# Gated linear attention and a mixture of experts: group 0 instead of group 1 takes K and Q through DRAM, and two groups sum |W|² by accumulating transfers

## The chip, the cores and the metric

The kernel runs on one core of one Trainium2 chip. Its engines are TensorE (PE, matrix products), VectorE (DVE, elementwise), ScalarE (ACT, functions and copies), GpSimd (POOL) and SyncE (SP); POOL and SP issue DMA transfers here. The metric is the device time of one execution in microseconds (us), lower is better. Everything is float32 in SBUF; the two matrix products of the experts use split float32r operands.

## The reference

Part one is a recurrence with a complex decay, over B=4 sequences, H=8 heads, S=768 steps and D=48 channels. Part two is a skip gate and a mixture of eight experts over the 3072 tokens that result.

```python
mag = np.sqrt(a_re * a_re + a_im * a_im)
scale = np.minimum(mag, 0.999) / (mag + 1e-06)
a_re_n, a_im_n = (a_re * scale, a_im * scale)
for t in range(S):
    ar, ai = (a_re_n[:, :, t, :, None], a_im_n[:, :, t, :, None])
    new_re = ar * S_re - ai * S_im
    new_im = ar * S_im + ai * S_re
    kv = np.einsum('bhd,bhe->bhde', k[:, :, t], v[:, :, t])
    S_re, S_im = (new_re + kv, new_im)
    y[:, :, t] = np.einsum('bhd,bhde->bhe', q[:, :, t], S_re)
...
do_compute = x @ w_skip > 0
e_idx = np.argmax(xc @ w_gate, axis=1)
h = np.maximum(xc[mask] @ w1[e], 0.0)
y[mask] = gate_w[mask, None] * (h @ w2[e])
out[do_compute] = xc + y
```

Here x is y with heads side by side (3072 x 384), xc its rows with a positive skip score, gate_w the largest softmax probability, and w1, w2 have an inner width of 1024.

## The kernel before, in words

The 768 steps are cut into 6 chunks of 128 steps, and two chunks make a group (NG = 3). Within a chunk the state is not carried: W is the running product of the decays from the middle of the chunk outwards, both halves (64 steps each) and both chunks of a group at once in the 128 partitions (2 halves x 2 chunks x 32 pairs of sequence and head). So a group is 64 steps of a serial string of small DVE instructions, the chain: multiply by the decay (L371), add the two products (L380). L365 copies the first decay of a group. A group has 8 pieces of 8 steps each, 24 pieces in all.

Ahead of the chain, gates normalise the decays (ACT L258 to L267, DVE L262, L266, L316, L324). Behind it, a consumer turns each piece of W into the two operands of the chunk's products: K times W (nw, L443) on one side of the middle and K over W on the other, and the same of Q. The inverse is the conjugate over |W|², so ACT squares W into ws (L438); the sum of the two squares is formed; ACT takes the power of the sum (L459, L460), and DVE refines it and forms iw (L462, L464, L467, L470). The sum is formed on PE, by two products with the identity into PSUM (sw, L452), except for a group's last piece, where DVE adds (L457).

The products contract over the channels, so K and Q have to lie with channels in partitions. For groups 0 and 2 each piece's nw and iw are transposed on PE (tp, L533) and copied by ACT (L540) into the two qk tiles of the group. Group 1 is the spilled group: its nw and iw, both K and Q, are written by POOL to a scratch in DRAM (keep, L492), read back by SP in natural order (nat, L503), and transposed by whole heads on PE (turn, tu L518) with ACT copies of 512 elements (L520). For group 0 only K goes to DRAM, since the state update contracts over time and needs it in natural layout (nat, L506).

A unit is one sequence's 8 heads of one chunk (c, b); 24 in all. It has scores (pa, PE L590, 16 products), mask (at, DVE L612, 2), the outputs (py, PE L667 and L670), the state update from natural K and V (ps, PE L656; RX on DVE; st by ACT L639), the copy and the gate's projection (px L675), and now and then a routing pass (small DVE instructions, then indirect scatters by POOL, xs). The spilled group's units read q and k after turn, and their K from the same natural tile.

The order of the instructions is written by generators under a class Order that keeps virtual times for the engines: chain, gates, consumers, units and weights each yield and are taken by priority and by lateness. The tile framework adds the waits and can hold an instruction on a buffer that is still read. The pools' buffer counts matter: qk has 2 buffers (a group's two tiles), nat and qkT 2 each. The consumers of group 1 go on at once; those of group 2, past the first piece, wait until 8 units are done, because their qk tiles reuse the buffers of group 0. After the attention come the routing's last pass and the experts.

The prediction counts work by stage and in the DVE order; "chain step" is the number of L380 instructions counted from the start (64 or 65 to a group, the last closing the group; 195 in all).

Of the kernel before, what the change touches and what calls it, by code (L numbers as in the profile page):

```python
# [9 lines left out]
F32 = mybir.dt.float32  # L10
# [4 lines left out]
ALU = mybir.AluOpType  # L15
# [4 lines left out]
B, H, S, D = 4, 8, 768, 48  # L20
DM = H * D
BH = B * H
C = 128
HC = 64
NCH = S // C
NG = NCH // 2
# [73 lines left out]
def vt(n, f=1.0):  # L100
    return (n / f + 65) / 0.96
# [8 lines left out]
class Kern:  # L110
# [229 lines left out]

    def chain(self, g):
        V = self.nc.vector
        qk = None
        if not self.spilled(g):
            qk = [self.qkp.tile([96, BH, 4, HC], F32, name=f"qk_{g}_{cc}", tag="qk") for cc in range(2)]
        self.QK[g] = qk
        prev = None
        for p in range(NP):
            i = g * NP + p
# [5 lines left out]
            n = LP + (1 if p == NP - 1 else 0)  # L355
# [33 lines left out]
    def consumers(self):  # L389
        while self.cons_done < NPC:  # L390
            g, u = divmod(self.cons_done, NP)
            if self.cq and (self.spilled(g) or u < 1 or self.units_done >= (g - 1) * 2 * B):
                yield from self.consume(*self.cq.pop(0))
            else:
                yield 0, 100

        self.rctx.close()
        self.m0 = self.pool(self.mctx, "m0", side="right")
        self.mr = self.pool(self.mctx, "mr", 2, side="right")
        self.t2 = self.pool(self.mctx, "t2", side="right")  # L400
        self.order.add(P_WEIGHTS, self.weights(0, self.m0), 3000)
# [30 lines left out]
    def consume(self, g, i, W, num, inv, jb, qk, wl):  # L432
# [13 lines left out]
        self.keep(g, nw, 1, 1, jb)  # L446
        yield o.wait(vt(2 * N), ts)
        w2, r0 = ws[:, :, 0], ws[:, :, 1]
        if wl is None:
            sw = self.ps_w.tile([128, LP, D], F32, name=f"sw_{i}", tag="sw")  # L450
            for c in range(2):
                nc.tensor.matmul(sw, self.ident, ws[:, :, c], start=(c == 0), stop=(c == 1))  # L452
            o.pe(1300, ts)
            cost = 0.0
        else:
            sw = w2
            V.tensor_tensor(w2, w2, r0, ALU.add)  # L457
            cost = vt(N)
# [9 lines left out]
        yield vt(N), 130  # L468
        iw = self.wk.tile([128, LP, 2, D], F32, name=f"iw_{i}", tag="nw")
        V.tensor_tensor(iw, bc(inv), Wm, ALU.mult)  # L470
        tq = self.trans(i, iw, 2, 1, jb, qk, vt(2 * N)) + 5000
        self.keep(g, iw, 1, 0, jb)
        self.keep(g, iw, 0, 1, jb)
        if wl is not None:
# [8 lines left out]

    def spilled(self, g):

        return g == 1

    def keep(self, g, src, side, q, jb):

# [5 lines left out]
    def nat(self, c, b):  # L495

        if c >= 2 * (NG - 1):
            return
        g, cc = divmod(c, 2)
        t = self.nats[c, b] = self.un.tile([C, H, 2, 2 * D], F32, name=f"nat_{c}_{b}", tag="nat")  # L500
        r = cc * BH + b * H
        if self.spilled(g):
            self.nc.sync.dma_start(t.rearrange("p h q d -> p (h q) d"),  # L503
                                   self.kq[g][r:r + H].rearrange("h q s d -> s (h q) d"))
        else:
            self.nc.sync.dma_start(t[:, :, 0], self.kq[g][r:r + H, 0].rearrange("h s d -> s h d"))  # L506

    def turn(self, c, b):

        nc = self.nc  # L510
        t = self.nats[c, b]
        qk = self.un.tile([96, H, 4, HC], F32, name=f"qkT_{c}_{b}", tag="qkT")
        for hh in range(2):
            hs = slice(hh * 4, hh * 4 + 4)
            for q in range(2):
# [83 lines left out]
    def unit(self, c, b):  # L599
# [88 lines left out]
            self.routes.append((self.lg_t, self.route1(c, b, lg, self.xa)))  # L688
        if c > 0:
            yield vt(768), 0  # L690
        nx = c * B + b + 2
        if nx < (c // 2 + 1) * 2 * B:
            self.nat(*divmod(nx, B))

# [8 lines left out]

    def units(self, g):
        self.nat(2 * g, 0)
        self.nat(2 * g, 1)
        self.unit_at(2 * g, 0)
        for cc in range(2):
            c = 2 * g + cc
# [169 lines left out]
    def attention(self):  # L879
        with ExitStack() as ctx:  # L880
# [1 line left out]
            P = lambda *a, **kw: self.pool(ctx, *a, **kw)  # L882
            self.rctx = ExitStack()
            self.ld, self.gt, self.wk = [self.pool(self.rctx, n, 2, side="right") for n in ("ld", "gt", "wk")]
            self.qkp, self.un, self.st = P("qk", 2), P("un", 2), P("st")
            self.ps_tp, self.ps_at = P("ps_tp", 2, space=PSUM), P("ps_at", 2, space=PSUM)
            self.ps_y, self.ps_s, self.ps_m = P("ps_y", 1, space=PSUM), P("ps_s", 1, space=PSUM), P("ps_m", 1, space=PSUM)
            self.ps_w = P("ps_w", 1, space=PSUM)
# [357 lines left out]
```

## Time and profile before

| | us |
|---|---|
| median of 3 runs | 538.61 |
| lowest, highest | 535.48, 540.12 |
| profiled execution, its own time | 543.87 |
| span of the profiled execution | 542.2 |

PE is busy 430.7 us of the span, DVE 412.1, ACT 291.8, POOL 88.3; the mean granted TensorE clock is 0.887. In a group row of the profile, "busy" is the union of a group's executions and the mean in ns that of one; PE's products overlap, so their pitch is shorter than their mean. A window row gives its bounds, its length, then for PE, PE's weight loads, DVE, ACT and POOL the busy us (and the instructions started), and last the granted TensorE clock, the share of the DMA engines and GB/s. In a waits row stand the total us, how many times, and the longest wait.

### The profile page before, as it was taken

Reading aid. Unit: us, or ns where it says so; the run is one execution under the profiler, and the core shown is the slowest. Engines: PE = TensorE matmul, PEld = TensorE weight load, DVE = VectorE, ACT = ScalarE, POOL = GpSimd, SP = SyncE. Lnnn points to the kernel's source line nnn. Section 1 sums busy time; section 2 is a strip of 40 time slices with the busy share of each in tenths; the row PEclk is TensorE's granted clock in tenths of the full one; section 3 lists DMA queues with packets and bytes.
Section 4 is the critical chain, followed back from the end, with each engine's and each line's share of the span. In section 5 each row is a group of like instructions: output and inputs, shape, how many; then the busy total and the mean of one; then the engine's idle time right before and its main releaser. Section 6 shows DMA issues by size and latency. Waiting matters only on the chain. (4 is left out here: it accounts for less than half of the span.)

```text
span 542.2 us, 10042 instructions
## 1 busy us (share of the span) xinstructions
PE 430.7 (79%) x3253; PEld 376.9 (70%) x3253; DVE 412.1 (76%) x1139; ACT 291.8 (54%) x658; POOL 88.3 (16%) x158
## 2 busy tenths in 40 slices
PE   0256446579989322899999998999998999999994
PEld 0134324479866201788778888998988999999994
DVE  2988999965999989789889847689469566866621
ACT  3657657714655554587778673332266454654410
POOL 4011011101132444000000300202112001120111
PEclk9966876667999765799999996799999999999998
DMA  4558777787988867858644325534659568666300
GB/s 85 113 113 179 176 151 169 159 163 178 230 196 195 197 152 168 186 113 194 135 112 110 96 67 179 145 113 119 219 175 312 189 209 273 182 196 226 105 20 28
DMA packets 160523, 85.72 MB, mean 158 GB/s; under 512 B 134491, under 2 KB 154463, under 8 KB 160464
## 3 DMA queue, kind: packets, MB, share of 16 engines
q1 hardware_dynamic: 155216, 70.93, 51.7%
q0 software_dynamic: 5248, 14.07, 9.6%
q8 instruction: 28, 0.46, 0.3%
q14 instruction: 31, 0.25, 0.1%
HBM read 61.84 MB, written 25.21 MB: 161 GB/s over the span
## 5 line engine op out<-in xcount | busy, mean ns | idle before, releaser
L452 PE MATMUL sw<-ws,ident 128*128 128x384 f32 x84 | 44.3, 664 | 37.9 <-ACT ws L438 37.9
L371 DVE TENSOR_TENSOR X<-W,ain 128x192 f32<-128x192 f32 x192 | 67.7, 352 | 2.9
L936 DVE TENSOR_TENSOR l<-r,h 128x768 fp32r<-128x768 f32 (+1 forms) x56 | 58.0, 1069 | 13.3 <-ACT h L935 13.2
L935 ACT CAST h<-r 128x768 fp32r<-128x768 f32 (+1 forms) x56 | 49.7, 925 | 17.6 <-DMA r<-in_moe_w_dram 12.7
L452 PEld LDWEIGHTS sw<-ws,ident 128*128 128x128 f32 x84 | 19.5, 257 | 50.6 <-issue 27.1
L1000 PE MATMUL ph<-xh,h 128*128 128x256 f32 x192 | 53.0, 282 | 0.6 <-issue 0.6
L1000 PE MATMUL ph<-xh,l 128*128 128x256 f32 x192 | 53.2, 282 | 0.0
L1002 ACT ACTIVATE hh<-ph 128x256 fp32r<-128x256 f32 x64 | 23.7, 382 | 53.8 <-PE ph L1000 53.8
L612 DVE TENSOR_TENSOR at<-pa,mask 128x512 f32<-128x512 f32 x48 | 32.7, 685 | 25.1 <-PE pa L590 21.4
L380 DVE TENSOR_TENSOR W<-X 128x96 f32<-128x96 f32 x192 | 48.7, 254 | 3.4
L1000 PE MATMUL ph<-xl,h 128*128 128x256 f32 x192 | 51.0, 281 | 0.0
L533 PE MATMUL tp<-ident,iw 128*96 128x128 f32 x128 | 23.6, 331 | 33.6 <-DVE iw L470 33.3
L1003 DVE SCALAR_TENSOR_TENSOR hl<-ph,hh 128x256 fp32r<-128x256 f32 x64 | 25.6, 418 | 29.2 <-ACT hh L1002 29.2
L540 ACT COPY qk<-tp 96x256 f32<-96x256 f32 x128 | 39.8, 369 | 11.4 <-PE tp L533 10.9
L1023 PE MATMUL po<-h,hh 128*128 128x384 f32 x128 | 43.8, 342 | 0.0
L739 POOL DMA_INDIRECT xs<-xa,sl x24 | 29.1, 1212 | 88.8 <-DVE l L936 20.5
L533 PEld LDWEIGHTS tp<-ident,iw 128*96 128x96 f32 x128 | 17.1, 151 | 37.9 <-issue 30.6
L1024 PE MATMUL po<-l,hh 128*128 128x384 f32 x128 | 43.3, 338 | 0.0
L667 PE MATMUL py<-at,vt 128*64 128x128 f32 x384 | 42.5, 298 | 0.0
L590 PE MATMUL pa<-qk 96*128 96x128 f32 x256 | 41.3, 316 | 1.0 <-DVE at L612 0.9
L1025 PE MATMUL po<-h,hl 128*128 128x384 f32 x128 | 39.5, 337 | 0.0
L590 PEld LDWEIGHTS pa<-qk 96*128 96x128 f32 x256 | 36.9, 222 | 3.2 <-PE py L670 1.1
(225 smaller groups left out, 1077.2 us busy)
## 6 DMA issues: line engine op xcount, KB each, us to landing
r<-in_moe_w_dram SPq DMA_DIRECT2D x24, 512.0 KB, 5.4
r<-in_moe_w_dram SPq DMA_DIRECT2D x32, 384.0 KB, 4.2
nat<-kq SPq DMA_DIRECT2D x8, 768.0 KB, 5.5
kq<-nw POOLq DMA_DIRECT2D x24, 192.0 KB, 3.4
kq<-iw POOLq DMA_DIRECT2D x24, 192.0 KB, 2.9
vt<-in_v_dram SPq DMA_DIRECT2D x24, 192.0 KB, 2.8
out_dram<-xa SPq DMA_DIRECT2D x24, 192.0 KB, 2.1
ain<-in_a_re_dram SPq DMA_DIRECT2D x90, 48.0 KB, 2.9
```

The lines of the kernel that those rows point to most:

```text
L371: V.tensor_tensor(X, prev.unsqueeze(1).to_broadcast([128, 2, 2, D]), windows(ain[:, j]), ALU.mult)
L380: self.cins = V.tensor_tensor(W[:, j, ::-1], X[:, :, 0], X[:, :, 1], ALU.add).ins
L452: nc.tensor.matmul(sw, self.ident, ws[:, :, c], start=(c == 0), stop=(c == 1))
L533: nc.tensor.transpose(tp[:, jj], src[:, s * 4 + jj], self.ident)
L540: nc.scalar.copy(o, tp[:, :, :, cc].rearrange("p j s b -> p b s j"))
L590: nc.tensor.matmul(pa[h // 4][:, h % 4], KT(h), QT(h), start=True, stop=True)
L667: PE.matmul(py[j * 64:j * 64 + 64, hp], vt_[:, 2 * hp + j], at[:, 2 * hp + j], start=True, stop=(c == 0))
L935: nc.scalar.copy(hi[:, ks], raw)
L936: nc.vector.tensor_tensor(lo[:, ks], raw, hi[:, ks], ALU.subtract)
L1000: pe = PE.matmul(ph, w[:, k, js], x[:, k], start=(n == 0), stop=(n == len(terms) - 1))
L1023: PE.matmul(po, hh[:, j, sl], w2h[:, j], start=(j == 0), stop=False)
L1024: PE.matmul(po, hh[:, j, sl], w2l[:, j], start=False, stop=False)
```

## The change

Group 0 becomes the spilled group, so its K and Q go through DRAM and are turned by whole heads, and group 1's pieces are transposed one by one. The pool of qk tiles has three buffers. Group 0 uses one of them (area): natural tiles lie in its first part, turned ones behind them, two of each. Groups 1 and 2 have the other two and then, for the second tile of group 2, the buffer that group 0's units have left or that chunk 2's units leave. The natural K of later units has a tile with a single buffer of its own, and is loaded one unit ahead instead of two. For the pieces of groups 1 and 2 the sum of the two squares is made by a transfer that POOL issues with addition at its target, ws onto ws; group 0 keeps PE's way. The delay of 5000 before the first units of a group is for the spilled group only, and the consumers of the last group go on after 12 units instead of 8.

```diff
--- before.py
+++ after.py
@@ -340,9 +340,12 @@
 
     def chain(self, g):
         V = self.nc.vector
-        qk = None
-        if not self.spilled(g):
-            qk = [self.qkp.tile([96, BH, 4, HC], F32, name=f"qk_{g}_{cc}", tag="qk") for cc in range(2)]
+        qk = [self.qkp.tile([128, BH * 4 * HC], F32, name=f"qk_{g}_{cc}", tag="qk")
+              for cc in range(1 if self.spilled(g) else 2)]
+        if self.spilled(g):
+            self.area, qk = qk[0], None
+        else:
+            qk = [t[0:96].rearrange("p (h k t) -> p h k t", h=BH, k=4) for t in qk]
         self.QK[g] = qk
         prev = None
         for p in range(NP):
@@ -389,7 +392,7 @@
     def consumers(self):
         while self.cons_done < NPC:
             g, u = divmod(self.cons_done, NP)
-            if self.cq and (self.spilled(g) or u < 1 or self.units_done >= (g - 1) * 2 * B):
+            if self.cq and (g < NG - 1 or u < 1 or self.units_done >= 3 * B):
                 yield from self.consume(*self.cq.pop(0))
             else:
                 yield 0, 100
@@ -446,7 +449,13 @@
         self.keep(g, nw, 1, 1, jb)
         yield o.wait(vt(2 * N), ts)
         w2, r0 = ws[:, :, 0], ws[:, :, 1]
-        if wl is None:
+        if g:
+
+            sw = w2
+            nc.gpsimd.dma_start(w2, r0, accum_op=ALU.add)
+            ts += 4000
+            cost = 0.0
+        elif wl is None:
             sw = self.ps_w.tile([128, LP, D], F32, name=f"sw_{i}", tag="sw")
             for c in range(2):
                 nc.tensor.matmul(sw, self.ident, ws[:, :, c], start=(c == 0), stop=(c == 1))
@@ -468,7 +477,7 @@
         yield vt(N), 130
         iw = self.wk.tile([128, LP, 2, D], F32, name=f"iw_{i}", tag="nw")
         V.tensor_tensor(iw, bc(inv), Wm, ALU.mult)
-        tq = self.trans(i, iw, 2, 1, jb, qk, vt(2 * N)) + 5000
+        tq = self.trans(i, iw, 2, 1, jb, qk, vt(2 * N)) + 5000 * self.spilled(g)
         self.keep(g, iw, 1, 0, jb)
         self.keep(g, iw, 0, 1, jb)
         if wl is not None:
@@ -483,7 +492,7 @@
 
     def spilled(self, g):
 
-        return g == 1
+        return g == 0
 
     def keep(self, g, src, side, q, jb):
 
@@ -497,19 +506,26 @@
         if c >= 2 * (NG - 1):
             return
         g, cc = divmod(c, 2)
-        t = self.nats[c, b] = self.un.tile([C, H, 2, 2 * D], F32, name=f"nat_{c}_{b}", tag="nat")
         r = cc * BH + b * H
         if self.spilled(g):
+            t = self.part(c, b, 0, H * 4 * D).rearrange("p (h q d) -> p h q d", h=H, q=2)
             self.nc.sync.dma_start(t.rearrange("p h q d -> p (h q) d"),
                                    self.kq[g][r:r + H].rearrange("h q s d -> s (h q) d"))
         else:
+            t = self.un.tile([C, H, 1, 2 * D], F32, name=f"kt_{c}_{b}", tag="kt", bufs=1)
             self.nc.sync.dma_start(t[:, :, 0], self.kq[g][r:r + H, 0].rearrange("h s d -> s h d"))
+        self.nats[c, b] = t
+
+    def part(self, c, b, o, n):
+
+        o += (c * B + b) % 2 * n
+        return self.area[:, o:o + n]
 
     def turn(self, c, b):
 
         nc = self.nc
         t = self.nats[c, b]
-        qk = self.un.tile([96, H, 4, HC], F32, name=f"qkT_{c}_{b}", tag="qkT")
+        qk = self.part(c, b, 2 * H * 4 * D, H * 4 * HC)[0:96].rearrange("p (h k t) -> p h k t", h=H, k=4)
         for hh in range(2):
             hs = slice(hh * 4, hh * 4 + 4)
             for q in range(2):
@@ -688,7 +704,7 @@
             self.routes.append((self.lg_t, self.route1(c, b, lg, self.xa)))
         if c > 0:
             yield vt(768), 0
-        nx = c * B + b + 2
+        nx = c * B + b + (2 if self.spilled(c // 2) else 1)
         if nx < (c // 2 + 1) * 2 * B:
             self.nat(*divmod(nx, B))
 
@@ -703,7 +719,8 @@
 
     def units(self, g):
         self.nat(2 * g, 0)
-        self.nat(2 * g, 1)
+        if self.spilled(g):
+            self.nat(2 * g, 1)
         self.unit_at(2 * g, 0)
         for cc in range(2):
             c = 2 * g + cc
@@ -882,7 +899,7 @@
             P = lambda *a, **kw: self.pool(ctx, *a, **kw)
             self.rctx = ExitStack()
             self.ld, self.gt, self.wk = [self.pool(self.rctx, n, 2, side="right") for n in ("ld", "gt", "wk")]
-            self.qkp, self.un, self.st = P("qk", 2), P("un", 2), P("st")
+            self.qkp, self.un, self.st = P("qk", 3), P("un", 2), P("st")
             self.ps_tp, self.ps_at = P("ps_tp", 2, space=PSUM), P("ps_at", 2, space=PSUM)
             self.ps_y, self.ps_s, self.ps_m = P("ps_y", 1, space=PSUM), P("ps_s", 1, space=PSUM), P("ps_m", 1, space=PSUM)
             self.ps_w = P("ps_w", 1, space=PSUM)
```

Three places show what stands where in the order. Names: tp a piece's transposes (the first number is the piece), tpe the transposed decays at a group's end, sw the sum on PE, tu turned natural K or Q (chunk, sequence, half of the heads, K or Q), pa scores, ps state product, py outputs, at masked scores; the last number is only a running one.

PE, before, from the end of group 0's transposes to the first units of chunk 0:

```order
L533 MATMUL tp_7_1_2_1045<-ident_59,iw_7_1036 96x128 x4
L452 MATMUL sw_8_1115<-ws_8_1108,ident_59 128x384 x2
L551 MATMUL tpe_0_1057<-ident_59,e_0_1055 96x128 x2
L590 MATMUL pa_0_0_0_1134<-qk_0_0_193 128x128 x4
L590 MATMUL pa_0_0_1_1135<-qk_0_0_193 128x128 x4
L656 MATMUL ps_0_0_1172<-vt0_164,nat_0_0_1129 96x48 x8
L590 MATMUL pa_0_1_0_1162<-qk_0_0_193 128x128 x4
L667 MATMUL py_0_0_1183<-at_0_0_1147,vt0_164 64x128 x4
```

PE, after, at the same place:

```order
L461 MATMUL sw_6_748<-ws_6_729,ident_59 128x384 x2
L567 MATMUL tpe_0_870<-ident_59,e_0_868 96x128 x2
L549 MATMUL tp_8_0_0_910<-ident_59,nw_8_908 96x128 x4
L549 MATMUL tp_8_1_0_917<-ident_59,nw_8_908 96x128 x4
L534 MATMUL tu_0_0_0_0_940<-ident_59,qk_0_0_193 96x128 x4
L534 MATMUL tu_0_0_0_1_946<-ident_59,qk_0_0_193 96x128 x4
L672 MATMUL ps_0_0_1035<-vt0_164,qk_0_0_193 96x48 x8
L534 MATMUL tu_0_0_1_0_952<-ident_59,qk_0_0_193 96x128 x4
L534 MATMUL tu_0_0_1_1_958<-ident_59,qk_0_0_193 96x128 x4
L606 MATMUL pa_0_0_0_965<-qk_0_0_193 128x128 x4
```

The transposes of group 0's pieces are gone; piece 8 of group 1 and the turning of unit 0_0 stand ahead of the first scores, and the turning of each next unit between the units' products.

DVE, before, the end of the chain:

```order
L371 TENSOR_TENSOR X_23_8_3658<-W_23_3542,ain_23_3151 128x192
L443 TENSOR_TENSOR nw_22_3498<-num_22_3331,W_22_3341 128x768
L380 TENSOR_TENSOR W_23_3542<-X_23_8_3658 128x2x48
L428 TENSOR_TENSOR wend_112<-es_2_3679 128x48
L470 TENSOR_TENSOR iw_22_3553<-inv_22_3332,W_22_3341 128x768
L612 TENSOR_TENSOR at_3_3_3486<-pa_3_3_0_3433,mask_72 128x512
L612 TENSOR_TENSOR at_3_3_3486<-pa_3_3_1_3434,mask_72 128x512
```

DVE, after, where the last unit of chunk 3 stands now (piece 21 of 0 to 23):

```order
L374 TENSOR_TENSOR X_21_1_3322<-W_21_3297,ain_21_2835 128x192
L479 TENSOR_TENSOR iw_19_3176<-inv_19_2850,W_19_2859 128x768
L383 TENSOR_TENSOR W_21_3297<-X_21_1_3322 128x2x48
L628 TENSOR_TENSOR at_3_3_3328<-pa_3_3_0_3207,mask_72 128x512
L628 TENSOR_TENSOR at_3_3_3328<-pa_3_3_1_3208,mask_72 128x512
L374 TENSOR_TENSOR X_21_2_3330<-W_21_3297,ain_21_2835 128x192
```

The masked products of unit 3_3 stood behind the last step of the chain; now two and a half pieces of the chain come after them.

POOL, after, in group 1 (before, the rows of L455 are not there):

```order
L501 DMA kq1_121<-iw_8_1072 64x768
L455 DMA ws_9_1170<-ws_9_1170 128x8x48
L501 DMA kq1_121<-nw_9_1172 64x8x96
L734 COPY xa_1_1449<-tok_101 128x4
L455 DMA ws_10_1334<-ws_10_1334 128x8x48
L237 MEMSET ain_15_1805 64x144
L501 DMA kq1_121<-iw_9_1312 64x768
L501 DMA kq1_121<-nw_10_1336 64x8x96
L455 DMA ws_11_1627<-ws_11_1627 128x8x48
```

The accumulating transfer of each piece stands in POOL's order between the writes of K to DRAM, and ACT's logarithm (L468) waits for it.

## The prediction

> **What bounds the kernel now.** I read the page's table of engines first, then the busy time by stage, then DVE's waits, and last the rows at the places that the change touches. The page's chain of waits is no help: it holds only the last output transfer. Over the whole run PE and DVE are nearly level:
>
> ```profile
> PE 430.7 (79%) x3253; PEld 376.9 (70%) x3253; DVE 412.1 (76%) x1139; ACT 291.8 (54%) x658; POOL 88.3 (16%) x158
> ```
>
> That average hides the stages. These windows are cut at the end of group 0's recurrence (93.9), where the first units begin (104.8), where the K and Q of group 1 are about to come back from DRAM (214.7), at the end of group 2's recurrence (311.3), at chunk 4's first masked product (326.7) and at the end of the attention (376); per engine they give busy microseconds:
>
> ```profile
> 12.60:104.80 92.20, 44.73 (x158) 29.89 (x159) 84.36 (x225) 61.02 (x156) 11.22 (x22) 0.73 0.69 148
> 104.80:214.70 109.90, 74.13 (x571) 60.16 (x570) 94.18 (x282) 54.15 (x123) 32.72 (x48) 0.80 0.81 187
> 214.70:311.30 96.60, 95.22 (x774) 76.83 (x775) 83.41 (x227) 69.97 (x172) 4.70 (x7) 0.95 0.61 135
> 311.30:326.70 15.40, 14.68 (x148) 12.88 (x145) 7.79 (x35) 10.75 (x33) 0.88 (x2) 1.00 0.31 76
> 376.00:542.00 166.00, 154.32 (x1149) 152.23 (x1145) 100.13 (x224) 74.41 (x137) 24.66 (x29) 0.99 0.54 176
> ```
>
> I call the first four A, B, C and T (the tail). The recurrence is a serial string on DVE; everything else is fitted between its steps. DVE is idle 92.2-84.4 = 7.8 us in A, 109.9-94.2 = 15.7 in B, 96.6-83.4 = 13.2 in C and 15.4-7.8 = 7.6 in T, 44.3 in all. C is the one stage where PE is full (95.2 of 96.6). What DVE waited for, in A, in 104.8 to 136.4 (the front of B), in 214.7 to 245 (the front of C) and in T, in us, times and longest:
>
> ```profile
> DVE sq L266 <- ACT t L264: 4.2, 7, 1.3
> ...
> DVE at L612 <- PE pa L590: 10.6, 5, 3.4
> ...
> DVE at L612 <- PE pa L590: 4.0, 4, 3.1
> ...
> DVE at L612 <- PE pa L590: 3.7, 2, 3.0
> DVE iw L420 <- PE tp L533: 2.0, 1, 2.0
> ```
>
> Two thirds of the idle time in B and nearly half of that in T are masked products waiting for PE's scores. At the front of B, PE itself was slow: between 112 and 120 it was busy without a break at a granted clock of 0.51, and before that it waited once for K from DRAM:
>
> ```profile
> 93.90:104.80 10.90, 4.79 (x18) 3.75 (x19) 10.48 (x30) 7.59 (x22) 1.52 (x3) 0.50 0.61 146
> 112.00:120.00 8.00, 8.00 (x48) 6.89 (x47) 3.21 (x7) 1.33 (x3) 0.07 (x1) 0.51 0.62 112
> 180.00:214.00 34.00, 5.74 (x19) 2.62 (x18) 32.11 (x110) 16.59 (x36) 16.30 (x24) 0.61 0.71 168
> ...
> PE ps L656 <- DMA nat<-kq: 3.2, 1, 3.2
> ```
>
> The third row shows the other imbalance: from 180 to 214 PE has 5.7 us of work, and then C in which it has no gap.
>
> **The change, part by part.** DVE executes nearly the same instructions before and after (two adds, L457 in groups 1 and 2, go). So I take DVE's work up to 326.7 as fixed and ask only what becomes of its 44.3 idle us. The sum is made against the profiled execution: 543.87 us, span 542.2, 1.7 outside it. That run is 5.3 above the median of the runs, 538.61; I carry the difference over to the median.
>
> *Group 0 is spilled instead of group 1.* The rows of what moves:
>
> ```profile
> L533 PE MATMUL tp<-ident,iw 128*96 128x128 f32 x128 | 23.6, 331 | 33.6 <-DVE iw L470 33.3
> L540 ACT COPY qk<-tp 96x256 f32<-96x256 f32 x128 | 39.8, 369 | 11.4 <-PE tp L533 10.9
> ...
> L518 PE MATMUL tu<-ident,nat 128*96 128x128 f32 x128 | 19.7, 291 | 1.0 <-DMA nat<-kq 0.8 <-ACT qkT L520 0.3
> ...
> L520 ACT COPY qkT<-tu 96x512 f32<-96x512 f32 x32 | 18.1, 583 | 7.7 <-PE tu L518 7.7
> ```
>
> In A, ACT loses group 0's 64 copies (39.8/2 = 19.9 us of its 61.0) and PE the transposes. DVE's 4.2 us behind ACT at L266 are there because ACT was late; I take half back: **-2** (bounds -4.2 and 0).
>
> B takes those copies for group 1 and also the 32 copies after the turn. ACT goes from 54.2 by 19.9+18.1 to 92; PE gains about 14 us for the turn (eight turning matmuls in a row took 1.04 us, below, and one lasts 0.29, so each adds (1.04-0.29)/7 = 0.107, times 128) and 14 for group 1's transposes, and loses the sums of some seven pieces (7 x 1.46 = 10): 74.1+18 = 92. Both would be some 90% of a B shortened to about 102. They stay behind DVE's 94 only just, and in the order the last units of B lie nearer to each other.
>
> ```profile
> 246.05 1.46 PE L452 MATMUL sw<-ws,ident 128*128 128x384 f32 x4
> 247.34 1.04 PE L518 MATMUL tu<-ident,nat 128*96 128x128 f32 x8
> ```
>
> What B gains: the first masked product stands behind chain step 90 instead of 77, so steps of the recurrence and group 0's last piece run while PE turns, where now DVE has only masked products left to wait for. Of the 10.6 us I take 7.5 back: **-7.5** (bounds -10.6, all of it, and +3, if ACT's and PE's 92 us become the stage's string). The 3 us that remain are the cold start, which nothing in the change removes: PE goes into B after an A with 20 us less on it, and the row of 93.9 to 104.8 already has 0.50.
>
> The Trainium skill, page "TensorE: Matmul & The Clock Gate", Part 1, says that PE falls to half clock after an idle window of about 3.4 us and needs about as long of busy time to come back. The trace agrees on the fall (0.50 and 0.61 in thin stretches), but not on the return: 0.51 lasted through 8 us of unbroken work here. By the rule the cold start would cost half of 3.4 us of work (an estimate from that page), and the 3 us kept in B would be 1.7; by the rows at 0.51 it costs 4 us of 8.
>
> *C.* Units 2_0 to 3_3 find their Q and K turned in SBUF, so the turn (14 us of PE) and the sums of seven pieces (27 matmuls, about 10 us) leave PE's 95.2. First unit: now its at comes at 228.59, after a write, a read and a turn:
>
> ```profile
> 211.70 1.26 POOL L492 DMA_DIRECT2D kq<-iw  x2
> ...
> 215.74 2.25 SPq L503 DMA_DIRECT2D nat<-kq  x2
> ...
> 228.59 0.69 DVE L612 TENSOR_TENSOR at<-pa,mask 128x512 f32<-128x512 f32 x1 [3.08 <-PE pa L590]
> ```
>
> In the new order the eight units lie between chain steps 146 and 172 instead of 146 and 195 and beyond. That squeezes: in that stretch PE has the units' work and the early pieces' transposes, 95.2-14-10 = 71, less three pieces' transposes that come later (3 x 16 x 0.107 = 5), some 65 us; DVE has, by its order at the rows' durations, some 49 us there and 35 us after it, where PE is nearly idle. So DVE waits about 16 us in the squeezed stretch, against 13.2 in the whole of C now: **+3** (bounds -5, if units start some 10 us earlier than DVE needs and PE works ahead, and +16, the next paragraph).
>
> *One buffer for the natural K of a later unit, one unit ahead.* A load can start only when the unit before has read its K, and on SP it stands behind loads of ain, num and inv which wait for DVE to free their tiles. A read of K and Q or K alone, and the wait on SP:
>
> ```profile
> nat<-kq SPq DMA_DIRECT2D x8, 384.0 KB, 5.3
> ...
> SPq L227 <- DVE W L380: 4.5, 7, 2.4
> SPq L587 <- PE py L667: 3.8, 2, 2.5
> ```
>
> The read lands 5.3 us after issue; 65 us over eight units is 8 us a unit, so it is hidden with 2.8 us to spare, if SP is not blocked for longer. SP's longest wait on the recurrence now is 2.4. I take **0**. Two such waits in each unit would make 2 x 2.4+5.3 = 10.1 us, 2 more than a unit has, and 8 x 2 = +16 over the stage: the upper end. Who waits if it fails: the state matmuls (L656), the scores queued behind them on PE, then DVE.
>
> *Sums of |W|² by an accumulating transfer, 15 pieces.* Removed: PE's 4 matmuls each, at 1.46 us warm, already counted. Added: 15 transfers on POOL, each with 192 KB added from one half of a tile to the other, in 192-byte rows. No row shows an accumulating transfer. The nearest: POOL's own writes of 192 KB, its issue time (1.26 for two, above), a load with the same rows (per transfer KB and us to landing), a scatter of the routing, and PE's way with a cold PE:
>
> ```profile
> kq<-iw POOLq DMA_DIRECT2D x24, 192.0 KB, 2.9
> vt<-in_v_dram SPq DMA_DIRECT2D x24, 192.0 KB, 2.8
> ...
> 203.66 2.37 POOL L739 DMA_INDIRECT xs<-xa,sl  x1 [1.09 <-DMA xs<-xa,sl]
> ...
> 213.67 2.93 PE L452 MATMUL sw<-ws,ident 128*128 128x384 f32 x4 [8.78 <-ACT ws L438]
> ```
>
> So about 3 to 6 us from the square to the logarithm (the upper end with an indirect scatter of routing ahead in POOL's order), against 1.5 to 2.9 for PE's way. The logarithm waits in ACT's queue, and behind it the copies of transposed pieces, of states and of outputs, for which PE waits; DVE waits for the power of the sum (L462, 464). In DVE's new order five of the 15 pieces have under 6.5 us of other DVE work between the square and its use, the others 8 to 14. Between nothing and +18 (2 us on nine pieces) I take **+4.5**, those five at 0.9: nearer to nothing, since the rows' 2.8 and 2.9 are nearest.
>
> The Trainium skill, "DMA: Bandwidth & Descriptors", Anatomy of one DMA, gives a transfer issued by GpSimd about 2 us plus its bytes at 436 GB/s, an estimate of 2.45 us here; the trace's 2.9 is near it, though the page doesn't say what adding costs. By 2.45 the 4.5 would be about 3.
>
> *T.* Between the recurrence's end and chunk 4's first unit DVE now still has units 3_2 and 3_3 and a routing pass, because they come after the recurrence in the order. They move ahead of it. The 3.7 us at L612 and 0.8 of smaller waits go; the 2.0 at L420, the last piece's transposes, stays: **-4.5** (bounds -5.6 and 0). The next units then begin with a PE that has idled; at 0.65, this stretch has it now:
>
> ```profile
> 326.70:340.00 13.30, 11.64 (x75) 11.27 (x74) 10.13 (x22) 5.40 (x8) 2.15 (x2) 0.65 0.49 165
> ```
>
> I cost that at 0; a start at half clock is at most 11.6 x 0.15/0.5 = +3.5. The expert layers (166 us) are unchanged.
>
> Sum: -2 -7.5 +3 +0 +4.5 -4.5 = **-6.5**. Profiled execution 543.9-6.5 = 537.4; median 538.6-6.5 = **532.1**.
>
> **The rivals.**
> 1. *DVE's work becomes the only bound.* Waits at L266, at L612 in B and in T go entirely, PE in C runs ahead: -4.2 -10.6 -5 -4.5, while the accumulating transfers cost 4.5 and the late K's or the cold clock 3.5: -16, **522**. For it: PE idles 28 us between 180 and 214 and loses 24 us in C, so it has room. Against: the same trace has PE slow at 0.51 just when it is asked to begin. Chance 0.2.
> 2. *One K buffer and SP's queue hold PE.* Each of eight units in the squeezed stretch starts its state matmuls 2 us late; this decides from the point where SP is blocked for more than 2.8 us per unit. +16 on the sum: 532.1+16 = **548**, slower. For it: SP's 2.4 us waits, and the single read that was late cost PE 3.2. Against: only one of eight such reads made PE wait until now. Chance 0.16.
> 3. *The accumulating transfers are slow.* At 2 us beyond the cover on nine of 15 pieces it is +18 instead of +4.5, so 532.1+13.5: **546**, slower. It decides from the point where the way takes 8 us or so, the cover of the middle pieces. For it: POOL's in-order scatters. Against: POOL is busy 16%, and the longer half of the pieces has 8 to 14 us of cover. Chance 0.12.
> 4. *The gain doesn't arrive: the idle time moves.* B's DVE waits on ACT and PE at 92 us of load, C stays PE-bound: 0 in B, the rest as in the sum, 532.1+7.5: **540**. Chance 0.14.
>
> **How the numbers follow.** My forecast, 526 to 538 with 532.1 as its middle, has 0.38. About 1% (5.4 us) can be told from no change here. Faster by more: rival 1 whole and 0.22 of the forecast's 0.38, since its middle lies only just beyond 1%: 0.42. Slower by more: rivals 2 and 3, less 0.03 in which they are half as big, 0.25. Within: the other 0.33. The range 521 to 547 cuts off the far side of rival 1 and the upper part of rivals 2 and 3, about 0.2.
>
> **What would show it.** In the changed profile: waits at the masked product in the front of B 3 us rather than 10.6; the first unit of chunk 2 some 15 us sooner; the last unit of chunk 3 before the recurrence's end; PE idle at its end; and at the logarithm, ACT waiting for a DMA, in sum under 10 us. I am wrong if the state matmuls wait for kt by more than 5 us together (rival 2), if ACT's wait on the accumulate is over 20 (rival 3), or if B is no shorter (rival 4).

## The result, and the profile after

The changed kernel is slower: 560.0 us median (556.9 to 563.8) against 539.4, a ratio of 1.041 with a 95% interval of 1.030 to 1.052. The forecast was 532.1 with a range to 547. Ratios leave disturbed runs out, here and below, so they need not be the quotient of the medians. The profiled execution took 556.9 us. The page's first table, after:

```profile
PE 402.2 (72%) x3197; PEld 357.0 (64%) x3197; DVE 414.3 (75%) x1138; ACT 293.7 (53%) x658; POOL 115.1 (21%) x173
```

PE has lost 28.5 us, as it should, and DVE's work has stayed (412.1 before). So the prediction's way of counting can be kept: DVE's work up to chunk 4's first masked product is fixed, and the time is what becomes of its idle time. Its four stages are here cut exactly at chain steps 1, 65, 130 and 195 and at that masked product. (The 195 steps are 192 instructions of L380 and the three copies at L365.) These are the windows of the changed kernel, with the columns as before: after the bounds come the length, PE, PE's weight loads and then DVE's busy time.

```profile
12.20:96.60 84.40, 20.46 (x28) 8.21 (x28) 73.49 (x197) 40.03 (x82) 18.07 (x33) 0.61 0.74 174
96.60:204.40 107.80, 84.42 (x729) 73.20 (x731) 89.74 (x243) 77.18 (x187) 24.25 (x32) 0.83 0.95 192
204.40:339.10 134.70, 95.63 (x809) 79.70 (x806) 107.92 (x326) 77.53 (x204) 37.27 (x31) 0.81 0.65 118
339.10:343.40 4.30, 4.20 (x26) 3.38 (x25) 1.31 (x11) 2.92 (x10) 1.96 (x2) 0.75 0.14 44
```

And those of the kernel before, from a later execution that took 532.6 us (label e11 below), since the one of the prediction lay 5 us over its median:

```profile
11.90:91.80 79.90, 40.08 (x138) 26.75 (x139) 72.84 (x194) 51.79 (x132) 9.67 (x19) 0.70 0.67 147
91.80:200.30 108.50, 76.81 (x588) 61.90 (x586) 93.32 (x272) 57.48 (x134) 26.65 (x42) 0.80 0.79 185
200.30:308.10 107.80, 95.56 (x775) 75.84 (x777) 96.12 (x268) 75.72 (x185) 11.21 (x17) 0.90 0.63 144
308.10:323.60 15.50, 14.78 (x148) 12.98 (x145) 8.09 (x37) 10.81 (x34) 1.14 (x2) 1.00 0.29 81
```

DVE's idle time is length less busy: 7.1, 15.2, 11.7 and 7.4 before, 41.4 in all; 10.9, 18.1, 26.8 and 3.0 after, 58.8. That is 17.4 us more idle and 2 us more work, and chunk 4 begins 19.8 us later (343.4 against 323.6). The rest of the 24 us between the two executions comes after, where nothing was changed; that part took between 207 and 220 us in the traces of this case, so an execution's time alone doesn't tell where a change acts.

What DVE waited for from 12 to 345 us, after:

```profile
DVE ws L471 <- ACT ws L469: 24.1, 12, 5.7
DVE sq L266 <- ACT t L264: 8.5, 8, 2.3
DVE at L628 <- PE pa L606: 6.1, 7, 2.0
```

And before, in e11, from 12 to 327 us:

```profile
DVE at L612 <- PE pa L590: 15.9, 14, 3.4
DVE sq L266 <- ACT t L264: 7.1, 11, 1.5
DVE ws L462 <- ACT ws L460: 2.0, 2, 1.1
```

The masked product's wait for PE has fallen as forecast, from 15.9 to 6.1. The wait at L471 (L462 before), the first use of the power of |W|², has gone from 2.0 to 24.1. Behind it stand ACT's logarithm and, behind that, the accumulating transfer, by its own line's view:

```profile
L455 POOL DMA_DIRECT2D ws<-ws x15: 1547/1597/1736, 109.8 to 325.2; - x15
...
  ACT ws L468: 24.8, 10
...
DMA to landing us min/median/max: 5.0/5.7/7.6
```

Each occupies POOL for 1.6 us and lands 5.7 us after its start (medians). ACT's 24.8 us of waiting is over the 20 that the prediction gave as the sign of its rival 3. The longest wait, at piece 19, shows how a piece's way looks (start, length, engine, line; POOL, then ACT, then DVE):

```profile
271.71 1.55 POOL L455 DMA_DIRECT2D ws<-ws  x1 [1.14 <-ACT ws L441]
...
270.58 0.84 ACT L441 ACTIVATE ws<-W 128x768 f32<-128x768 f32 x1
...
277.37 0.61 ACT L468 ACTIVATE ws<-ws,col 128x384 f32<-128x384 f32 x1 [2.92 <-DMA ws<-ws]
...
278.25 0.52 ACT L469 ACTIVATE ws<-ws 128x384 f32<-128x384 f32 x1
...
278.80 0.56 DVE L471 TENSOR_TENSOR ws<-ws 128x384 f32<-128x384 f32 x1 [5.74 <-ACT ws L469]
```

From the square's end (271.42) to the logarithm's start 6 us pass, and 7.4 to L471. DVE ran out of what stood ahead of L471 in its order and stood still for the last 5.74 of them, the chain with it. Over all 15 pieces, the rows of these lines give 6.8 us in the median from the square's end to the logarithm's start (5.4 to 15.9); over the 15 last pieces in e11, it is 3.5 (1.7 to 7.6).

### The profile page after: what moved, and what is told of

The parts are those of the page before. It is cut to its first block, busy times and chain, and to the rows that moved or that the text cites. A ratio compares the mean times of both kernels' runs of the same rounds, so it can differ in the third digit from the quotient of the medians.

```text
span 555.2 us, 9960 instructions
## 1 busy us (share of the span) xinstructions
PE 402.2 (72%) x3197; PEld 357.0 (64%) x3197; DVE 414.3 (75%) x1138; ACT 293.7 (53%) x658; POOL 115.1 (21%) x173
## 5 line engine op out<-in xcount | busy, mean ns | idle before, releaser
L461 PE MATMUL sw<-ws,ident 128*128 128x384 f32 x28 | 20.5, 885 | 70.1 <-ACT ws L441 70.1
L461 PEld LDWEIGHTS sw<-ws,ident 128*128 128x128 f32 x28 | 8.2, 324 | 81.2 <-ACT ws L441 56.5
L756 POOL DMA_INDIRECT xs<-xa,sl x24 | 33.2, 1385 | 115.4 <-DMA xs<-xa,sl 23.9
L606 PE MATMUL pa<-qk 96*128 96x128 f32 x384 | 55.2, 292 | 2.4 <-DVE at L628 2.1
L606 PEld LDWEIGHTS pa<-qk 96*128 96x128 f32 x384 | 49.6, 202 | 6.7 <-DVE at L628 2.7
L549 PE MATMUL tp<-ident,iw 128*96 128x128 f32 x128 | 22.3, 319 | 30.2 <-DVE iw L479 29.9
L683 PE MATMUL py<-at,vt 128*64 128x128 f32 x384 | 40.8, 288 | 0.6 <-DVE at L628 0.6
L549 PEld LDWEIGHTS tp<-ident,iw 128*96 128x96 f32 x128 | 16.6, 148 | 33.8 <-ACT ws L441 24.3
```

The source lines that it names most:

```text
L549: nc.tensor.transpose(tp[:, jj], src[:, s * 4 + jj], self.ident)
L606: nc.tensor.matmul(pa[h // 4][:, h % 4], KT(h), QT(h), start=True, stop=True)
L683: PE.matmul(py[j * 64:j * 64 + 64, hp], vt_[:, 2 * hp + j], at[:, 2 * hp + j], start=True, stop=(c == 0))
```

## The experiments

Theory 1: the accumulating transfers cost the time. Theory 2: moving the spilled group does. Each run has DVE's idle time by stage, worked out as above from its own trace; group 0 is up to chain step 65, and so on, and the tail reaches to chunk 4's first masked product.

| kernel | median us | ratio to before (95%) | idle in groups 0, 1, 2, tail | idle / work |
|---|---|---|---|---|
| before (execution of 532.6) | 534.1 | 1 | 7.1, 15.2, 11.7, 7.4 | 41.4 / 270.3 |
| changed | 560.0 | 1.041 (1.030 to 1.052) | 10.9, 18.1, 26.8, 3.0 | 58.8 / 272.4 |
| e1 changed, PE's sums | 537.3 | 0.999 (0.995 to 1.004) | 11.3, 12.8, 14.9, 2.9 | 41.9 / 272.2 |
| e2 before, accumulating | 561.1 | 1.043 (1.035 to 1.052) | 7.2, 20.5, 34.4, 5.7 | 67.8 / 272.8 |
| e3 changed, DVE adds | 539.5 | 1.006 (0.998 to 1.014) | 11.5, 12.3, 9.9, 2.2 | 35.9 / 277.8 |
| e4 changed, long rows | 544.8 | 1.012 (1.002 to 1.021) | 10.6, 14.9, 18.5, 2.2 | 46.2 / 270.0 |
| e5 before, Q written for group 0 | 537.4 | 1.006 (1.004 to 1.008) | 9.7, 9.7, 14.5, 7.8 | 41.7 / 269.8 |
| e7 changed, POOL adds | 538.0 | 1.007 (1.003 to 1.012) | 10.7, 11.0, 5.6, 2.7 | 30.0 / 279.6 |
| e10 before, DVE adds in group 2 | 535.2 | 0.995 (0.991 to 0.999) | 7.5, 17.1, 13.6, 0.8 | 39.0 / 273.9 |
| e12 e10 and idle products | 526.6 | 0.980 (0.972 to 0.988) | 7.2, 12.8, 8.9, 0.8 | 29.7 / 273.5 |
| e13 changed, order told | 570.4 | 1.066 (1.059 to 1.074) | 11.1, 19.5, 33.2, 4.5 | 68.3 / 271.5 |
| e14 before and idle products | 535.2 | 0.988 (0.978 to 0.998) | 7.2, 13.8, 11.1, 7.4 | 39.5 / 270.3 |

The medians of the kernel before, beside which each was timed, were 534.0 to 535.9. e6, e8 and e9 had one execution each and stand below. The traces of e1, e10 and e14 are of executions above their medians (548.1, 538.5 and 538.8). e1's surplus lies after chunk 4's first masked product: that part took 220 us with a granted clock of 0.93, against 207 and 1.00 in e11.

**e1 and e2: one part at a time.** e1 takes the transfers out of the changed kernel, e2 puts them into the one before.

```diff
 # e1, on the changed kernel
-        if g:
-            sw = w2
-            nc.gpsimd.dma_start(w2, r0, accum_op=ALU.add)
-            ts += 4000
-            cost = 0.0
-        elif wl is None:
+        if wl is None:
 # e2, on the kernel before
+        if g:
+            sw = w2
+            nc.gpsimd.dma_start(w2, r0, accum_op=ALU.add)
+            cost = 0.0
-        if wl is None:
+        elif wl is None:
```

> The changed kernel with PE's sums in all three groups; the move of the spilled group, the three qk buffers and the single K buffer stay. Theory 1 (the accumulating transfers cost the time: in the changed kernel's trace DVE waits 24 us at L471 for ACT, and ACT 24.8 us for the transfers): most of the 24 us goes, some of it comes back as PE work, 536 to 546 us. Theory 2 (the move costs it: more DRAM writes beside group 0's loads, units squeezed before chain step 172): it stays above 552 us.

> The kernel before with the accumulating transfers alone, for the 15 pieces of groups 1 and 2 that take PE's way or DVE's add; group 1 stays spilled. Theory 1: 12 to 22 us slower than before, 551 to 561, with ACT waiting 15 to 30 us for the transfers. Theory 2: within 4 us of before, since PE in stage C gets 11 us lighter.

Theory 1 holds on both sides: without the transfers the changed kernel is no slower than the one before (0.999), and with them alone the one before is as slow as the changed one (1.043). The first row below is DVE's wait for the power in e1, which was 24.1 us with the transfers. In e2 DVE waits for the power as well (third row), and the masked product's wait also grew, from 15.9 in e11 (second row):

```profile
DVE ws L465 <- ACT ws L463: 5.1, 7, 1.8
...
DVE at L616 <- PE pa L594: 21.4, 12, 4.1
DVE ws L466 <- ACT ws L464: 18.4, 8, 3.9
```

So the accumulating transfers cost 23 to 27 us, and the move of the spilled group with its three buffers and single K buffer costs or gains nothing that can be measured (e1's interval is about 0.5% to either side).

**e3: DVE adds.** In the branch for groups 1 and 2:

```diff
-            nc.gpsimd.dma_start(w2, r0, accum_op=ALU.add)
-            ts += 4000
-            cost = 0.0
+            V.tensor_tensor(w2, w2, r0, ALU.add)
+            cost = vt(N)
```

> The changed kernel with DVE adding the two squares of the 15 pieces (0.47 us each on DVE in sequence, 7 us in all) in place of the transfers. Theory 1: ACT's and DVE's waits of 24 us go and 7 us of work come, 540 to 548. Theory 2: 555 to 567.

539.5, just under what theory 1 gave. DVE's work rises by 5.4 us (272.4 to 277.8), and its idle time falls by 22.9. Here an addition that lengthens DVE's string was far cheaper than a transfer that costs DVE no work at all.

**e4, e6, e8: what makes the transfer slow.** e4 lays the two squares out as two contiguous halves; e6 (short rows) and e8 (long ones) let DVE add and then copy the sum over the other half by a plain transfer, from which the logarithm reads.

```diff
 # e4
-ws = self.wk.tile([128, LP, 2, D], F32, ...)
+ws = self.wk.tile([128, 2, LP, D], F32, ...)
-        A.activation(ws, Wm, AF.Square)
+        A.activation(ws.rearrange("p c j d -> p j c d"), Wm, AF.Square)
 # e6, and with e4's layout e8
-            nc.gpsimd.dma_start(w2, r0, accum_op=ALU.add)
+            V.tensor_tensor(w2, w2, r0, ALU.add)
+            nc.gpsimd.dma_start(r0, w2)
-        A.activation(r0, sw, AF.Ln, bias=self.tiny)
+        A.activation(r0, r0 if g else sw, AF.Ln, bias=self.tiny)
```

> The changed kernel with the two squares laid out as two contiguous halves, so that a transfer has one row of 1536 bytes in each partition in place of eight of 192. If the short rows make the transfer slow (5.7 us to landing, median), it lands in 3 to 4 us and issues in 0.6 us in place of 1.6, and the time falls by 8 to 14 us, to 546 to 552. If the way is slow as such (issue, ring, completion), landing stays over 5 us and the time within 3 us of the changed kernel.

> The changed kernel, in which DVE adds the squares and POOL's transfer then copies the sum over the other half, without adding, in the same rows of 192 bytes, before the logarithm reads it: the transfer's shape stays and the adding goes. If the adding makes it slow, it lands in 3 to 4 us where the accumulating one takes 5.7 (median); if the short rows do, it lands in over 5 us.

> The same plain copy in rows of 1536 bytes. With the accumulating transfers in short rows (5.7 us) and long ones (3.8) it completes a table of two by two. If the adding costs nothing, 3.6 to 4.0 us; if it costs, 2.5 to 3.2 us.

The view of the transfer's line, in each: POOL's time in ns (least, median, most) and the time to landing. e4, then e6, then e8:

```profile
L455 POOL DMA_DIRECT2D ws<-ws x15: 887/951/1029, 109.3 to 313.0; - x15
...
DMA to landing us min/median/max: 3.0/3.8/4.9
```

```profile
L456 POOL DMA_DIRECT2D ws<-ws x15: 882/911/952, 111.4 to 325.0; - x15
...
DMA to landing us min/median/max: 3.5/4.0/5.2
```

```profile
L456 POOL DMA_DIRECT2D ws<-ws x15: 546/572/604, 111.1 to 316.8; - x15
...
DMA to landing us min/median/max: 2.1/3.4/5.3
```

With the changed kernel's 1.6 us and 5.7 the table is complete. Adding costs 1.7 us to landing in short rows (4.0 to 5.7) and 0.4 in long ones (3.4 to 3.8); short rows cost 0.6 without adding and 1.9 with it. e8's 3.4 lies between the two ranges expected for it. So adding and short rows each cost little alone, and much together, and POOL's own time goes the same way (0.57, 0.91, 0.95, 1.60). Why is open. Long rows bring back 15 of the 25 us (544.8), a little more than expected. The last 10 (6 by the ratio) stay: DVE still waits 10.4 us at L471 in e4, and from the square's end to the logarithm's start the median is 6.4 us, against 4.5 with PE's sums (e1). e6 and e8 took 555.2 and 553.1 us in one execution each; they put DVE's addition and a transfer in series and were made for the table only.

**e5: the first group.** The changed kernel's group 0 ended 4 us later, and so did that of e1 and e3.

```diff
-        if g < NG - 1 and (q == 0 or self.spilled(g)):
+        if g < NG - 1 and (q == 0 or self.spilled(g) or g == 0):
```

> The kernel before, in which group 0 writes Q as well as K to DRAM (16 more writes of 192 KB that nobody reads); nothing moves. In the changed kernel and in e1 and e3 group 0's chain ends (step 65) some 4 us later, at 96.6 to 97.0 against 92.3, and ACT waits longer for its inputs. Theory 1 (the writes crowd the loads of decays, K and Q on the DMA engines): step 65 moves to 95 to 97 and DVE's wait at L266 grows by 3 us. Theory 2 (the new order in the first group, without transposes on PE, or a colder PE): step 65 stays at 92 to 93. The time as a whole: 0 to +4 us.

Step 65 came at 94.6, against 91.8 to 93.1 in three traces of the kernel before and 96.1 to 97.1 in the six kernels of the table with the move; DVE's wait at L266 was 6.6 us (4.2 before, 7.6 after). So the 16 writes explain about half of the delay, and theory 1 is half right. e5 is 0.6% slower in all, but its chunk 4 begins at 323.5, as in e11 (323.6), so that 0.6% isn't traced to group 0. ACT waits longer for its inputs, as this row of the kernel after shows:

```profile
ACT sq L258 <- DMA num<-in_k_dram: 18.4, 7, 4.9
```

Before, that row read 15.0, 7, 4.6. With the wait for the decays' loads it is 19.2 us before, 23.0 after and 23.0 in e5, although in e5 more of it is the decays'. The other half of the delay stays open.

**e7: POOL adds.**

```diff
-            nc.gpsimd.dma_start(w2, r0, accum_op=ALU.add)
-            ts += 4000
+            nc.gpsimd.tensor_tensor(w2, w2, r0, ALU.add)
```

> The changed kernel, in which POOL itself adds the two squares of the 15 pieces (an elementwise addition of 128x384) in place of the transfers. POOL is busy 21%, and nothing lands late: if POOL's addition takes 1 us or less and does not slow DVE, DVE's wait for the power of the sum falls from 24 to under 6 us and the time to 533 to 541. If POOL's addition takes 2 us or holds up DVE, 541 to 548.

DVE's wait for the power is 1.3 us, its idle time the lowest of the changed kernels (30.0), and yet it is no faster than before: DVE's work is 279.6 us, 7.2 more than in the changed kernel, although it executes the same instructions. The rows show where (DVE, then POOL):

```profile
109.83 1.16 DVE L374 TENSOR_TENSOR X<-W,ain 128x192 f32<-128x192 f32 x1
111.02 0.26 DVE L383 TENSOR_TENSOR W<-X 128x96 f32<-128x96 f32 x1
111.31 0.36 DVE L374 TENSOR_TENSOR X<-W,ain 128x192 f32<-128x192 f32 x1
...
109.60 1.17 POOL L455 TENSOR_TENSOR ws<-ws 128x384 f32<-128x384 f32 x1 [1.44 <-ACT ws L441]
```

The multiplication that meets POOL's addition takes 1.16 us, the next one 0.36. The time lies in the range expected for an addition that doesn't slow DVE, although POOL's did.

**e10, e12, e14: a better kernel.** e10 is the kernel before with the sums of group 2's seven middle pieces on DVE; e12 is e10 with 30 products on PE whose result nobody reads, where PE pauses before group 1; e14 is the kernel before with these products alone.

```diff
 # e10
-        if wl is None:
+        if wl is None and g < NG - 1:
 # e12 and e14, ahead of the transposes of group 0's last iw
+        if i == NP - 1:
+            warm = self.ps_w.tile([128, LP, D], F32, name="warm", tag="sw").rearrange("p j d -> p (j d)")
+            for _ in range(30):
+                nc.tensor.matmul(warm[:, 0:96], self.ident, nw[:, 0].rearrange("p c d -> p (c d)"), start=True, stop=True)
```

> The kernel before, with the sums of group 2's seven middle pieces made by DVE in place of PE; nothing else. PE is the bound of stage C and loses 10 us there, DVE gains 7 x 0.47 = 3.3 us of work. If PE's relief counts, 3 to 6 us faster than before; if DVE's string sets the end, 0 to 3 us slower.

> The kernel of e10 (the one before with DVE's sums in group 2's middle pieces) with 30 idle products of PE (identity with a piece of nw, never read) between group 0's last transposes, where PE has nothing to do for 5.7 us. They leave no result. If the low clock at the first units comes from that pause, PE starts group 1 at 1.0 in every execution, DVE's idle time in group 1 is 8 to 11 us, and the median falls by 2 to 6 us below e10's. If not, the median stays within 1.5 us of e10's.

> The kernel before with the 30 idle products of e12 alone (they leave no result); sums as before. e12 was 8.6 us below e10 in the median, and both changes lie in it. If the idle products do it by themselves, 527 to 531 us, and DVE idles less in group 1 than the 15.2 to 15.8 us of the three traces of the kernel before. If the two only work together, within 2 us of before.

e10 is 0.1% to 0.9% faster, on the short side of what was expected of PE's relief. Its trace doesn't show that relief: the masked product's wait is 16.6 us (15.9 in e11), and idle time goes from the tail (7.4 to 0.8) while group 2 has 1.9 more. In its order, all 32 masked products of the first four chunks come before the chain's end, where 30 did. So where e10's gain comes from stays open. e12 beats both kernels of this case, with 526.6 us and a ratio of 0.980 (0.972 to 0.988). e14 alone is 0.988 with a wide interval (its four runs lay between 525.3 and 540.5), so which of its two expectations holds isn't settled. The two edits' ratios multiply to 0.983, so they may simply add up. The mechanism is shown only in part. The windows from 93.9 to 136 in e12:

```profile
93.90:104.80 10.90, 10.64 (x77) 10.57 (x78) 10.18 (x31) 7.55 (x20) 1.24 (x2) 0.79 0.60 145
104.80:112.00 7.20, 4.77 (x40) 4.02 (x39) 6.58 (x19) 3.11 (x10) 1.23 (x2) 1.00 1.02 243
112.00:120.00 8.00, 8.00 (x47) 6.94 (x46) 3.33 (x8) 0.47 (x1) 1.22 (x2) 0.51 0.75 159
120.00:136.00 16.00, 16.00 (x128) 14.85 (x127) 12.22 (x30) 8.25 (x19) 1.97 (x5) 0.82 0.81 194
```

PE no longer begins the group at 0.50, but between 112 and 120 the clock is at 0.51 again, and DVE idles 12.8 us in group 1, not the 8 to 11 expected. The expectation on the clock has fallen in that point, though the time fell, and by more than expected (8.6 us below e10's median, not 2 to 6).

**e9 and e11: the kernel before, again.** e9 and e11 are the unchanged kernel, for further traces.

> The kernel before, unchanged, for a second trace beside the experiments' own. The trace on which the prediction rests has DVE idle for 44.6 us from the first chain step to chunk 4's first masked product, 15.8 of them in group 1, where PE ran at a clock of 0.51 to 0.72. Theory 1 (that idle time belongs to the kernel): 42 to 46 us again, and a hole of about 10 us at the first units. Theory 2 (part of it belonged to that one execution, whose clock was low just there; e5, nearly the same kernel, had 9.7 in group 1): 36 to 40, with 8 to 11 in group 1, so that the move had less to take back than the prediction counted on.

> The kernel before once more, for a trace of an execution near its median: the two traces so far took 543.9 and 541.9 us, with PE at a clock of 0.50 from the first units on and 15.7 us of idle time on DVE in group 1. Theory 2 (the slow clock at the first units belongs to some executions): an execution near 535 has PE at 0.9 to 1.0 between 112 and 120, 8 to 11 us of idle DVE in group 1, and reaches chunk 4's first masked product at 319 to 322 in place of 326.7. Theory 1: 15 us of idle again, and the time is lost elsewhere.

e9 took 541.9 us, with 15.7 us of idle time in group 1; e11 took 532.6, with 15.2 and this row:

```profile
112.00:120.00 8.00, 8.00 (x51) 6.89 (x49) 4.09 (x10) 1.80 (x3) 1.13 (x2) 0.54 0.68 125
```

Theory 2 of these two falls: the idle time at the first units belongs to the kernel and was there to be won.

**e13: does the order know of the transfer?** In the changed kernel nothing reads ts after the 4000 is added to it.

```diff
             nc.gpsimd.dma_start(w2, r0, accum_op=ALU.add)
-            ts += 4000
+            yield 0, 5600
             cost = 0.0
```

> The changed kernel, in which the generator of a piece yields for 5600 ns between the transfer and the logarithm (in the changed kernel the 4000 added to ts is never read). If the time was lost because the planner counted the transfer at nothing, other work now comes before the logarithm on ACT and before the power's use on DVE, DVE's wait at L471 falls from 24 to under 12 us and the time to 545 to 552. If a piece's way is simply longer than the work that may lie beside it (three W buffers, consumption in order), the wait stays over 18 us and the time within 5 us of the changed kernel's 560.

570.4 us, slower still. DVE's wait at L471 falls only to 18.5, other waits rise, and idle time in group 2 goes to 33.2:

```profile
DVE ws L471 <- ACT ws L469: 18.5, 12, 3.8
DVE at L628 <- PE pa L606: 11.2, 8, 3.1
DVE at L628 <- PE py L683: 5.8, 2, 4.5
```

The wait stays over 18 us, as the second expectation had it, but neither had the time rise by 10. A piece's way grew no longer: from the square's end to L471 it takes 8.3 us in the median, against 9.0 in the changed kernel. What grew are the waits at the masked product, 17.0 us in these rows against 6.8. So an order that reckons with the transfer in this way doesn't rescue it. That the three W buffers and the consumption in order set the limit is argued from the code, not shown.

## Why the prediction was wrong

**The step that failed is the accumulating transfers' term, "Between nothing and +18 ... I take +4.5".** Its size was wrong, not its mechanism: the chain of waits named there (transfer, logarithm on ACT, DVE's L471) is the one in the trace. By e1 and e2 the term is 23 to 27 us, beyond its upper bound. The way from the square to the logarithm, put at 3 to 6 us, took 5.4 to 15.9, 6.8 in the median. Two things in it were wrong. First, the rows taken as nearest, at 2.8 and 2.9 us to landing, were of plain transfers; the kind in question took 5.7, and e4, e6 and e8 show that adding and short rows each cost little alone and much together. Second, the cover, a piece's "other DVE work" between the square and its use: it was counted along the order and taken to hide the wait of ten pieces. DVE waited at L471 eleven times after group 0, 2.2 us each on average, not five times at 0.9. With 24.1 in place of 4.5 the sum reads -6.5+19.6 = +13, or 552; the rest of the way to 560.0 is the move, below.

**Group 0: -2, measured +3.3, in e1 +3.7.** The sign was wrong. DVE's idle time there rose from 7.1 to 8.0 in the three traces of the kernel before to 10.6 to 11.5 in all six kernels of the table that move the spilled group. ACT did lose its 64 copies, but Q's 16 additional writes were not costed in that stage at all; e5 finds about half of it there.

**Group 1: -7.5 at the masked product.** The wait did fall, from 10.6 over the group to 5.9 in the changed kernel and 2.0 in e1, there by more than the 7.5 forecast. But in e1 the group's idle time fell by only 2.4 to 3 us (15.2 or 15.8 to 12.8). In its place came waits for ACT: 4.6 us at L266 (0.3 before) and 2.2 for the power (1.1 before). This is the heavier ACT that the prediction had only in its upper bound. Rival 4 ("the idle time moves") is what e1 shows for this stage.

**Group 2: +3 for the squeeze, 0 for the single K buffer.** In e1 the idle time is 14.9, against 11.7, 13.6 and 15.5 in the three traces of the kernel before: from 1 us less to 3 more. So the +3 is neither confirmed nor refuted. The single buffer costs nothing: in the changed kernel nothing waits on the loads of kt, and the state products on PE waited only for ACT's states (2.0 us in the squeezed stretch). Rival 2 falls.

**Tail: -4.5.** Idle time 7.4 to 3.0, -4.4. Right.

With PE's sums (e1), then, the edits of the move come to +3.7 -3.0 +1.3 -4.7 = -2.7 of idle time against the prediction's own trace and +2 of work: nothing, as measured. The forecast's -11 for that part was 10 us too hopeful; with -0.7 there and +24.1 for the transfers the sum gives 562, against 560.0 measured. Rival 3, with 546 and a chance of 0.12, named the cause, but priced it at +18 and kept the -11 beside it.

**The rules drawn on.** The Trainium skill, "DMA: Bandwidth & Descriptors", Anatomy of one DMA, gave the estimate of 2.45 us for a transfer. Here the plain transfers took 3.4 to 4.0 us and the accumulating ones 3.8 and 5.7. The Trainium skill, "TensorE: Matmul & The Clock Gate", Part 1, has PE fall to half clock after an idle window of about 3.4 us. The 0.50 before group 1, with a pause of 5.7 us there, agrees. e12 doesn't: PE was busy for 10.6 of the 10.9 us to 104.8 and idle for only 2.4 of the next 7.2, and was at 0.51 again from 112 on.

## What to carry to other kernels

A transfer put in place of an instruction on a serial string can cost the string what of its latency nothing covers, however little work it takes from the engines: here PE gave up some 1.5 us of work per piece, the transfer took 5.7 us to landing, and the string waited up to 5.7 us for a piece. If no row of the trace shows the kind of transfer in question, its upper bound isn't that of the nearest plain one. Before removing work from an engine, compare the price of an addition on the string itself (5.4 us of DVE's work for 15 pieces here, e3) with every way around it.

## What the runs showed of the hardware

- An accumulating transfer of 192 KB from SBUF to SBUF in rows of 192 bytes held POOL for 1.6 us and landed after 5.7 (5.0 to 7.6). In rows of 1536 bytes it was 0.95 and 3.8; for plain copies 0.91 and 4.0 in the short rows, 0.57 and 3.4 in the long ones.
- An addition by POOL of 128x384 took 1.0 to 1.7 us, and DVE multiplications and additions of two SBUF operands that met it took longer (e7): X 1.16 us instead of 0.36, W 1.05 and once 1.70 instead of 0.25. The masked product, which reads PSUM and SBUF, kept its 0.69.
- PE's granted clock stood at 0.50 to 0.54 between 112 and 120, with PE busy for 7.9 or 8.0 of the 8 us, in all six traces of the kernel before, e10, e12 and e14; in e5, with the same order but for Q's writes, it was 1.00 there, with PE busy for 6.7 of the 8 us. What sets it is open.
